# A transformer block whose instruction order and PSUM banks come from a stored table

## The chip, the cores and the metric

The kernel runs on one core of a Trainium2 chip. The metric is the device time of one execution in microseconds, as the median of several runs. The engines are TensorE (PE), VectorE (DVE), ScalarE (ACT) and GpSimd (POOL); SyncE (SP) issues the DMA transfers. PSUM, into which PE writes, has eight banks here called 0 to 7.

## The reference

One pre-layer-norm transformer block: attention with a sliding window, then a gated feed-forward network (FFN). Everything is float32; S = 2048 tokens, D = 448, 16 heads of 28, window W = 256, FFN width 1792.

```python
def _A_ref(x, wqkv, wo):                 # x: (1, 2048, 448)
    qkv = (x @ wqkv).reshape(B, S, 3, H, Dh).transpose(2, 0, 3, 1, 4)
    q, k, v = qkv[0], qkv[1], qkv[2]
    scores = einsum("bhqd,bhkd->bhqk", q, k) * Dh ** -0.5
    mask = (i - j >= 0) & (i - j < W)
    p = softmax(where(mask, scores, -1e9))
    o = einsum("bhqk,bhkd->bhqd", p, v)
    return o.transpose(0, 2, 1, 3).reshape(B, S, D) @ wo

def _B_ref(x, w_gate, w_up, w_down):
    return (gelu(x @ w_gate) * (x @ w_up)) @ w_down

h  = x + _A_ref(layernorm(x), A_wqkv, A_wo)
h2 = h + _B_ref(layernorm(h), B_w_gate, B_w_up, B_w_down)
```

## The kernel before

**How the program is made.** The kernel isn't written in the order in which it runs. Python functions record 6,036 operations in a list `L` (class `Lists`): each has an engine (`pe`, `dve`, `act`, `pool`, `sp`, or `py` for steps that only mark a point), an assumed cost and latency, a key, the data that it reads and writes, and the PSUM banks that it uses, at first as abstract `Bank` objects of a kind. By engine they are 3,324 for PE, 998 for DVE, 890 for ACT, 400 for POOL and 419 for SP. One operation may emit several instructions: an `attend` emits all its small matmuls.

**What sets the order.** `Lists.run` (L141) is a list scheduler: it keeps a clock for each engine, takes at each step the operation that can start earliest (by the key where several can), and gives an abstract bank a real one when its first operation starts, from those that `allowed` (L1534) names for its kind. Emission in this order fixes the order on each engine, since an engine's queue is in order, and it fixes the banks. `Lists.refine` (L338) runs this 110 times with changed keys and keeps the best by the model's time, `Lists.replay` (L253) adding random delays; `Lists.latest` (L291) computes late start times for new keys. All this happens while the kernel is built. Where the model shows a gap of more than 0.1 us on PE, `idle` (L1562) puts filler into it: transposes of the identity into a free bank (line L1573), allowed in the first 26 us of the model's time and from 235 to 330 us.

**The work.** Two passes p = 0, 1 over head groups, in each four chunks c of 512 tokens:
- `layer_norms` and `normalise`: statistics on DVE, scaling, PE transposes (L554), a split into a high and a low part. Matrix products use such high and low parts, so a product takes several matmuls; most are issued by the helper `mul` at line L496, and the splits stand at L499 (ACT) and L502 (DVE or POOL).
- `values` (matmuls of 224 columns) and `project_tile` (512 columns) make v, q and k; q and k go to DRAM and come back in another layout through `loads`, into the tile `ring`.
- `scores` (matmuls of 84 rows, read by DVE at L925 for row maxima), `maxima` (L952), `probs` (matmuls of 104 rows, read by ACT as exponentials at L997), `select` (POOL masks, L1008), `attend` (second products, L1027, banks 4 and 5), `drain`, and `output` (448 columns).
- the FFN: the first eight steps by `conv` and `down`, then `unit` and `down`. `unit` makes a two-by-two block of products from seven block products, with sums of token and weight blocks made by `combine` (DVE) and `record` (POOL, DVE). `down` accumulates groups on banks 4 to 7, read by DVE residual adds at L1297; `unit` uses banks 0 to 3.

In `allowed`, scores use banks 0 and 1 and probabilities banks 2 and 3 (bank 7 as well once the projections are through); the other products of attention use 6 and 7, and any that aren't in use yet or any more.

Of the kernel before, what the change touches and what calls it, by code (L numbers as in the profile page):

```python
# [62 lines left out]
SLOW = 9.0  # L63
WARM = 26.0
THIN = (235, 330)
# [3 lines left out]
WAKE = {"py": 0.0, "pe": 0.25, "dve": 0.025, "act": 0.025, "pool": 0.1, "sp": 0.02}  # L69
EASE = {"py": 0.0, "pe": 0.05, "dve": 0.04, "act": 0.04, "pool": 0.05, "sp": 0.02}  # L70


def mm(n):
    return max(n / 2400 + 0.004, 0.112)


ROUNDS = 110
SEED = 3
HEAT = 0.3
MIX = 0.8  # L80
COOL = 800
WIDE = 0.04
LATE = 0.015


class Op:
    __slots__ = ("eng", "cost", "lat", "key", "fn", "deps", "users", "left", "banks", "port", "ready", "start", "fin",
                 "size", "tag", "then", "took", "done", "rank")


class Bank:


    def __init__(self, kind):
        self.kind, self.k, self.left = kind, None, 0


class Lists:
# [3 lines left out]
    def __init__(self):  # L102
        self.ops, self.seen, self.open, self.all = [], {}, {}, {}

    def op(self, eng, cost, lat, key, fn, r=(), w=(), bank=None, port=False, size=0, tag=None, after=()):
        o = Op()
        o.eng, o.cost, o.lat, o.key, o.fn, o.port, o.size, o.tag = eng, cost, lat, key, fn, port, size, tag
        o.deps, o.users, o.ready, o.start = set(after), [], 0.0, None
        o.banks = () if bank is None else tuple(bank) if type(bank) is list else (bank,)
        for b in o.banks:  # L110
            b.left += 1
# [18 lines left out]
        for d in o.deps:  # L130
            d.users.append(o)
        self.ops.append(o)
        if tag is not None:
            self.open[tag] = self.open.get(tag, 0) + 1
            self.all.setdefault(tag, []).append(o)
        return o

    def fresh(self, tag):
        return self.open[tag] == len(self.all[tag])

    def run(self, allowed, idle, emit=False):  # L141

        E = ("py", "pe", "dve", "act", "pool", "sp")
        free = dict.fromkeys(E, START)
        free["py"] = 0.0
        lock = {"dve": 0.0, "pool": 0.0}
        bank_free = dict.fromkeys(range(8), 0.0)
        bus, dmas = 0.0, []
        cand = {e: [] for e in E}
        self.order = []  # L150
        self.open = {tag: len(l) for tag, l in self.all.items()}
        for i, o in enumerate(self.ops):
            o.left, o.ready, o.start, o.rank = len(o.deps), 0.0, None, (o.key, i)
            for b in o.banks:
                b.k, b.left = None, 0
            if not o.left:
                insort(cand[o.eng], (o.rank, o))
        for o in self.ops:
            for b in o.banks:
                b.left += 1  # L160
        n = len(self.ops)

        def start_of(e, o):
            t = max(free[e], o.ready)
            if o.port:
                t = max(t, lock["pool" if e == "dve" else "dve"] - 0.03)
            if e == "sp" and len(dmas) >= 8:
                t = max(t, dmas[-8])
            got = []
            for b in o.banks:  # L170
                if b.k is None:
                    ks = [k for k in allowed(b.kind) if bank_free[k] is not None]
                    if not ks:
                        return None, None
                    k = min(ks, key=lambda k: max(t, bank_free[k] + WAKE[e]))
                    t = max(t, bank_free[k] + WAKE[e])
                    got.append((b, k))
            return t, got

        def choice(e):  # L180
            found, now, most = [], free[e], None
            for _, o in cand[e]:
                if most is not None and o.ready > most:
                    continue
                t, got = start_of(e, o)
                if t is not None:
                    found.append((t, o, got))
                    if most is None or t + EASE[e] < most:
                        most = t + EASE[e]
                    if t <= now:  # L190
                        break
            return next((f for f in found if f[0] <= most), None)

        picks, stale = {}, set(E)
        while n:
            best = None
            for e in E:
                if e in stale:
                    picks[e] = choice(e)
                c = picks[e]  # L200
                if c is not None and (best is None or c[0] < best[0]):
                    best = c
            stale = set()
            if best is None:
                return None
            t, o, got = best
            e = o.eng
            if e == "pe" and t > free["pe"] + 0.1:
                until = idle(free["pe"], t, bank_free, emit)
                if until:  # L210
                    free["pe"] = until
                    stale = set(E)
                    continue
            del cand[e][bisect_left(cand[e], (o.rank,))]
            stale.add(e)
            if o.banks or o.tag is not None:
                stale |= {"pe", "dve"}
            if o.port:
                stale |= {"dve", "pool"}
            for b, k in got:  # L220
                b.k = k
                bank_free[k] = None
            o.start = t
            cost, lat = o.cost, o.lat
            if e == "sp":
                bus = max(bus, t + 1.2) + o.size * 0.0034 + (1.25 if len(dmas) == 2 else 0)
                lat = bus + 0.7 - t
                dmas.append(t + lat)
            if e == "pe" and t < SLOW:
                cost, lat = 2 * cost, lat + cost  # L230
            free[e] = t + cost
            o.fin = t + lat + (MARGIN if e == "sp" and t > 15 else 0)
            if o.port:
                lock[e] = t + cost
            self.order.append(o)
            if emit:
                o.fn()
            if o.tag is not None:
                self.open[o.tag] -= 1
            n -= 1  # L240
            for b in o.banks:
                b.left -= 1
                if not b.left:
                    bank_free[b.k] = max(o.fin, t + cost)
            for u in o.users:
                u.left -= 1
                u.ready = max(u.ready, o.start + cost if e == u.eng == "pe" else o.fin + WAKE[u.eng])
                if not u.left:
                    insort(cand[u.eng], (u.rank, u))
                    stale.add(u.eng)  # L250
        return max(o.fin for o in self.ops)

    def replay(self, rnd):  # L253

        E = ("py", "pe", "dve", "act", "pool", "sp")
        free, lock = dict.fromkeys(E, START), {"dve": 0.0, "pool": 0.0}
        bus, dmas, gone = 0.0, [], {}
        for o in self.order:
# [119 lines left out]
def block_kernel(ctx: ExitStack, tc, x, wqk_in, wv_in, wo_in, ffn_in, halves_in, out):  # L378
# [1155 lines left out]
    def allowed(kind):  # L1534
# [23 lines left out]
        if what == "att":  # L1558
            return [4 + i]
# [76 lines left out]
```

## Time and profile before

| | |
|---|---|
| median of 3 runs | 686.2 us (685.5 to 686.44) |
| span of the profiled execution, first to last instruction | 684.9 us |
| instructions | 12,356 |
| DMA | 89.67 MB, mean 131 GB/s |
| chain that ended last | PE 87%, DVE 6%, ACT 3%, DMA 2%, issue 1% |

The profiled execution's span lies 1.3 us under the median of the runs; the profile records no other time for it. "Busy" is the union of an engine's instruction intervals. PEld are weight loads, which run beside matmuls. A row of a group gives the line, engine, operation, names and shapes, then count, busy time, mean ns of one instruction, and idle time before them with what ended it. All names of matmul operands are those of tiles (`ring`, `proj`, `xT`, `wos`), whatever they hold at the time.

### The profile page before, as it was taken

How to read it: one execution, taken by the hardware profiler on the slowest of the kernel's cores; microseconds unless marked ns; L12 is line 12 of the kernel's file. 1: busy time of each engine (PE TensorE's matmuls, PEld its weight loads, DVE VectorE, ACT ScalarE, POOL GpSimd, SP SyncE). 2: the span in 40 equal slices, each digit the busy share in tenths (PEclk: the TensorE clock that was granted, in tenths of full speed). 3: DMA queues.
4: the chain of work that ended last, by engine and by line, in shares of the span. 5: the costliest groups of instructions: out<-in, count | busy, mean ns of one | idle time of the engine just before them, and what ended most of it. 6: DMA issues, size and time to landing. Idle time of an engine off the chain costs nothing.

```text
span 684.9 us, 12356 instructions
## 1 busy us (share of the span) xinstructions
PE 675.0 (99%) x4128; PEld 596.7 (87%) x4128; DVE 503.1 (73%) x1274; ACT 418.5 (61%) x908; POOL 295.9 (43%) x462
## 2 busy tenths in 40 slices
PE   8999999999999999999999999999999999999997
PEld 7898888888888888778998899899999999999997
DVE  7968979866587867884899998877667745645544
ACT  7758777776767788796555665644554543533331
POOL 5702544343445667645524465254654631501100
PEclk9999999999999999999999999999999999999999
DMA  8798655566547597633533432212112210111102
GB/s 289 230 304 265 224 190 177 164 186 199 178 143 226 162 248 202 170 75 84 152 87 103 117 108 75 85 53 78 65 53 91 66 53 15 38 53 68 54 1 107
DMA packets 92951, 89.67 MB, mean 131 GB/s; under 512 B 35224, under 2 KB 82008, under 8 KB 92888
## 3 DMA queue, kind: packets, MB, share of 16 engines
q1 hardware_dynamic: 92888, 88.89, 42.4%
q8 instruction: 32, 0.52, 0.3%
q14 instruction: 31, 0.25, 0.1%
HBM read 59.51 MB, written 29.36 MB: 130 GB/s over the span
## 4 chain that ended last, share of the span: by engine, by line
PE 87%; DVE 6%; ACT 3%; DMA 2%; issue 1%; POOL 0%; SPq 0%; DVEq 0%; ACTq 0%
PE bank L496 80%; PE bank L1027 6%; PE bank L554 1%; DVE X L502 1%; ACT ring L499 1%; DVE v L694 1%; DMA v<-xn 1%; DVE proj L502 1%; DMA q<-proj 1%; ACT xT L499 1%; DVE xT L502 1%; ACT proj L499 0%; ACT pp L997 0%; DVE mt L1342 0%; DVE bnst L531 0%
## 5 line engine op out<-in xcount | busy, mean ns | idle before, releaser
L496 PE MATMUL bank<-xT,proj 128*128 128x512 f32 x620 | 177.5, 384 | 0.0
L496 PE MATMUL bank<-ring 84*128 84x384 f32 (+5 forms) x618 | 155.1, 314 | 1.3 <-ACT pp L997 0.7
L925 DVE CUSTOM_DVE_ANT_0 mt<-bank,mt 128x384 bf16<-128x384 f32 (+2 forms) x256 | 129.0, 526 | 35.4 <-PE bank L496 30.3
L997 ACT ACTIVATE pp<-bank 128x384 f32<-128x384 f32 (+2 forms) x352 | 123.5, 389 | 44.6 <-PE bank L496 41.2
L496 PE MATMUL bank<-xT,ring 128*128 128x512 f32 x536 | 134.9, 380 | 0.2 <-ACT bank L1248 0.2
L496 PEld LDWEIGHTS bank<-ring 104*128 104x128 f32 (+2 forms) x618 | 109.6, 190 | 22.4 <-issue 5.8
L496 PE MATMUL bank<-ring,proj 128*128 128x448 f32 x628 | 127.5, 353 | 1.4 <-DVE hres L1297 1.4
L1008 POOL TENSOR_SCALAR_AFFINE_SELECT pp<-pp 128x512 f32<-128x512 f32 x120 | 74.6, 635 | 116.1 <-ACT pp L997 104.4
L496 PEld LDWEIGHTS bank<-xT,proj 128*128 128x128 f32 x620 | 113.7, 190 | 10.5 <-issue 0.4
L496 PEld LDWEIGHTS bank<-ring,proj 128*128 128x128 f32 x628 | 118.6, 189 | 4.5 <-ACT xT L499 1.8
L496 PEld LDWEIGHTS bank<-xT,ring 128*128 128x128 f32 x536 | 101.0, 189 | 13.7 <-ACT bank L1248 0.6
L1297 DVE TENSOR_TENSOR hres<-bank,hres 128x448 f32<-128x448 f32 x72 | 41.3, 622 | 26.8 <-PE bank L496 26.7
L496 PE MATMUL bank<-proj,xT 128*128 128x224 f32 x352 | 60.2, 276 | 0.3 <-DVE xT L502 0.2
L1259 ACT ACTIVATE v<-v 128x512 f32<-128x512 f32 x24 | 15.1, 630 | 69.9 <-DVE v L1241 69.9
L502 POOL TENSOR_TENSOR ring<-raw,ring 128x256 fp32r<-128x256 f32 (+2 forms) x42 | 38.4, 920 | 44.3 <-ACT ring L499 36.1
L496 PEld LDWEIGHTS bank<-proj,xT 128*128 128x128 f32 x352 | 53.3, 191 | 1.8 <-ACT proj L499 0.4
L1165 POOL TENSOR_TENSOR v<-raw 128x256 f32<-128x256 f32 x18 | 15.3, 851 | 87.0 <-DMA raw<-in_halves_dram 39.7
L502 DVE TENSOR_TENSOR proj<-v,proj 128x512 fp32r<-128x512 f32 (+1 forms) x56 | 44.0, 792 | 8.9 <-ACT proj L499 7.6
L496 PE MATMUL bank<-wos,ohl 128*128 128x448 f32 x192 | 50.2, 363 | 0.0
L499 ACT ACTIVATE proj<-v 128x512 fp32r<-128x512 f32 (+1 forms) x56 | 33.5, 601 | 24.3 <-DVE v L1267 13.5
L496 PE MATMUL bank<-X,ring 128*128 128x512 f32 x146 | 48.2, 379 | 0.0
L1165 POOL TENSOR_TENSOR raw<-raw 64x128 f32<-64x128 f32 (+1 forms) x90 | 46.3, 527 | 2.2
(116 smaller groups left out, 999.4 us busy)
## 6 DMA issues: line engine op xcount, KB each, us to landing
ring<-k SPq DMA_DIRECT2D x44, 336.0 KB
raw<-in_halves_dram SPq DMA_DIRECT2D x18, 640.0 KB
ring<-q SPq DMA_DIRECT2D x32, 336.0 KB
q<-proj SPq DMA_DIRECT2D x15, 448.0 KB
k<-proj SPq DMA_DIRECT2D x11, 448.0 KB
hres<-in_x_dram SPq DMA_DIRECT2D x16, 224.0 KB
xn<-xn SPq DMA_DIRECT2D x64, 56.0 KB
mt<-in_halves_dram SPq DMA_DIRECT2D x16, 224.0 KB
```

Of the source, the lines that this page charges most:

```text
L496: nc.tensor.matmul(o.rearrange("p (t h) -> p t h", h=2), w, mixed(m), **how)
L499: nc.scalar.activation(dst, src, AF.Copy)
L502: (eng or nc.vector).tensor_sub(dst, src, f(hi))
L554: nc.tensor.transpose(bank[b.k][:, n * 128:(n + 1) * 128], xn[i2][:, o:o + 128], ident)
L694: op("dve", 0.07 + n * 0.00104, 0.17 + n * 0.00104, key, lambda: nc.vector.tensor_tensor(out, a, b, op=op_), [*ar, *br, "mtfree"], w, port ...
L925: nc.vector.tensor_tensor_reduce(plain(junk[s % 2][:, o:384]), unmixed(bank[b.k][:, o:384]), plain(mask[:, o:384]), 1.0, -BIG, OP.add, OP. ...
L997: nc.scalar.activation(plain(pp[:, j, o * 128:o * 128 + n]), unmixed(bank[b.k][:, 0:n]), AF.Exp, scale=SCALE)
L1008: nc.gpsimd.affine_select(a, a, pattern=[[0, 4], [-cm, 128]], compare_op=op_, fill=0.0, base=0, channel_multiplier=cm)
L1027: nc.tensor.matmul(bank[b.k][32 * j:32 * j + DH + 1, lo * 128:(hi + 1) * 128], v[:, 4 * c - 2 + m, g % 2, j, :], pp[:, j, at[m] * 128:(at[ ...
L1165: op("pool", 0.14 + n * 0.00215, 0.18 + n * 0.00215, key, lambda: nc.gpsimd.tensor_tensor(out, a, b, op=OP.subtract), [*ar, *br], w, port= ...
L1259: op("act", 0.485, 0.608, key + 11, lambda: nc.scalar.activation(A, A, AF.Gelu_apprx_tanh), ta, ta)
L1297: op("dve", 0.533, 0.626, key + 3 * q + 3, lambda t=t, b=banks[q]: nc.vector.tensor_tensor(plain(hres[:, t, :]), unmixed(bank[b.k][:, 0:D] ...
```

## The change

`run`, `replay`, `latest`, `refine`, `allowed` and `idle` go, with their constants and the clocks of class `Op`. The functions that record the operations stay. A new method `play` reads a stored table, `PLAN`: 16-bit words, first one bank for each of the 926 bank groups in the order of recording, then the order. A word below 6,036 is the number of an operation, which is emitted; one above is a filler transpose into that bank.

```diff
+    def play(self, plan, warm):
+
         n = len(self.ops)
...
+        words = memoryview(zlib.decompress(base64.b85decode(plan))).cast("H")
+        banks = list(dict.fromkeys(b for o in self.ops for b in o.banks))
+        for b, k in zip(banks, words):
+            b.k = k
+        done = set()
+        for w in words[len(banks):]:
+            if w >= n:
+                warm(w - n)
+                continue
+            o = self.ops[w]
+            assert o.deps <= done
+            o.fn()
+            done.add(o)
+        assert len(done) == n
...
-    L.refine(allowed, idle)
-    L.run(allowed, idle, True)
+    def warm(k):
+        nc.tensor.transpose(bank[k][:, 0:128], ident, ident)
+
+    L.play(PLAN, warm)
```

The recorded costs change in two places (`mm(n)` loses its floor of 0.112 us, and `project_tile` its added 0.002 us), but nothing reads costs any more.

What the table holds, read off by decoding its words against the recorded list, beside the order and banks of before:

| | before | table |
|---|---|---|
| filler transposes | 84 | 32 |
| of these behind the 119th PE operation or filler | 49 | 0 |
| PE order from the first `unit` product on (1,524 operations) | | the same, place by place |
| neighbours kept in the order: PE, DVE, ACT, POOL, SP | | 2,001 of 3,323; 173 of 997; 149 of 889; 140 of 399; 70 of 418 |
| median and largest move in the order: DVE, ACT, POOL, SP | | 2 and 37; 2 and 53; 1 and 17; 2 and 30 |
| banks of the 256 scores | 0 and 1 in 250, 7 in 6 | 0 to 3, 6 and 7 in 31 to 52 each |
| banks of the 352 probability products | 2 and 3 in 329, 7 in 23 | 0 to 3, 6 and 7 in 39 to 69 each |
| a score's bank used last by a probability product, or the reverse | 7 | 245 |
| five or fewer PE instructions (operations and fillers) between a bank's last writer and the next group in it: scores | 24 | 51 |
| the same: probability products | 131 | 62 |
| banks of `attend`, `down` and `unit` | | the same |

In the table's order, residual adds of `down` in the later FFN stand in DVE's queue behind up to 3.7 us (by the recorded costs) of other DVE work that comes after their last matmul; in the order of before there is none for most of them.

434 lines of the change are left out of this document (142 added, 292 removed).

## The prediction

> **What bounds the kernel now.** I read the page's first lines, then stretches of the span, then the instructions of single stretches by their shape.
>
> ```profile
> span 684.9 us, 12356 instructions
> PE 675.0 (99%) x4128; PEld 596.7 (87%) x4128; DVE 503.1 (73%) x1274; ACT 418.5 (61%) x908; POOL 295.9 (43%) x462
> ```
>
> PE looks busy for 99% of the span, which would leave 9.9 us to any reordering. That reading is wrong here: a matmul counts as busy until its modelled end, and two that overlap hide the wait between their starts. So I ask how much time the matmuls of a stretch need when they follow each other closely, and compare that with the stretch. The next fence has four stretches, with busy time and counts of each engine, then the granted clock.
>
> ```profile
> 80.00:140.00 60.00, 60.00 (x465) 51.31 (x464) 51.73 (x169) 44.80 (x115) 26.06 (x36) 1.00 0.59 192
> 235.00:330.00 95.00, 93.70 (x695) 76.40 (x694) 69.66 (x208) 77.82 (x198) 59.33 (x84) 1.00 0.59 156
> 330.00:380.00 50.00, 48.50 (x238) 44.11 (x236) 45.72 (x113) 27.27 (x50) 18.96 (x31) 1.00 0.42 116
> 380.00:680.00 300.00, 299.88 (x1459) 275.41 (x1460) 200.95 (x343) 142.80 (x257) 113.31 (x176) 1.00 0.20 62
> ```
>
> From 380 us PE has 0.12 us of idle time in 300 us, and DVE, the next engine, is 67% busy. A closely packed piece of it, by the timeline (start, length, instructions), and one group of the attention's second products from the chain of waits:
>
> ```profile
> 406.44 2.43 PE L496 MATMUL bank<-ring,proj 128*128 128x448 f32 x12
> 408.71 1.03 PE L496 MATMUL bank<-xT,proj 128*128 128x512 f32 x4
> 409.57 0.38 PE L496 MATMUL bank<-X,proj 128*128 128x512 f32 x1
> 248.77 1.43 PE bank L1027 x24
> ```
>
> Twelve matmuls of 448 columns start in 408.71 - 406.44 = 2.27 us, 0.189 us each; four of 512 in 0.86 us, 0.215 each. Both are 0.422 ns a column. A second product costs 1.43 / 24 = 0.060 us. With these two prices, the end of attention, where output products and the first FFN products run beside it:
>
> ```profile
> L496 PE MATMUL bank<-xT,proj 128*128 128x512 f32 x114 | 32.3, 385 | 0.0
> L496 PE MATMUL bank<-ring 84*128 84x384 f32 x59 | 19.6, 355 | 0.2
> L496 PE MATMUL bank<-wos,ohl 128*128 128x448 f32 x72 | 17.7, 363 | 0.0
> L496 PE MATMUL bank<-ring 104*128 104x384 f32 x39 | 13.4, 361 | 0.8 <-ACT pp L997 0.7
> L496 PE MATMUL bank<-ring 104*128 104x256 f32 x36 | 10.2, 301 | 0.2
> L1573 PE MATMUL bank<-ident 128*128 128x128 f32 x46 | 8.9, 275 | 0.0
> L1027 PE MATMUL bank<-pp,v 128*29 128x384 f32 x80 | 8.4, 491 | 0.0
> L496 PE MATMUL bank<-ring 104*128 104x128 f32 x36 | 8.3, 253 | 0.1
> L496 PE MATMUL bank<-proj,xT 128*128 128x224 f32 x44 | 7.8, 277 | 0.0
> L1027 PE MATMUL bank<-pp,v 128*29 128x256 f32 x80 | 6.1, 379 | 0.0
> L1027 PE MATMUL bank<-pp,v 128*29 128x128 f32 x80 | 4.1, 278 | 0.0
> L952 PE MATMUL bank<-one,mhl 128*72 128x128 f32 x8 | 1.9, 239 | 0.0
> L496 PE MATMUL bank<-proj 128*128 128x448 f32 x1 | 0.4, 352 | 0.0
> ```
>
> Columns without L1573 and L1027: 114 x 512 + 98 x 384 + 73 x 448 + 44 x 224 + 36 x 256 + 44 x 128 = 153,408, or 64.8 us. The 240 second products add 14.3 us. PE needs 79.1 of these 95 us and **loses 15.9 us, 17%**. Line L1573, 46 transposes of the identity, is filler in that lost time, not work. The same count in the middle of attention:
>
> ```profile
> L496 PE MATMUL bank<-xT,proj 128*128 128x512 f32 x62 | 20.1, 385 | 0.0
> L496 PE MATMUL bank<-ring 84*128 84x384 f32 x61 | 19.9, 339 | 0.0
> L496 PE MATMUL bank<-wos,ohl 128*128 128x448 f32 x48 | 13.2, 363 | 0.0
> L496 PE MATMUL bank<-ring 104*128 104x384 f32 x32 | 10.2, 334 | 0.0
> L496 PE MATMUL bank<-proj,xT 128*128 128x224 f32 x44 | 7.8, 273 | 0.0
> L496 PE MATMUL bank<-ring 104*128 104x256 f32 x27 | 7.7, 290 | 0.0
> L1027 PE MATMUL bank<-pp,v 128*29 128x384 f32 x48 | 5.0, 491 | 0.0
> L496 PE MATMUL bank<-ring 104*128 104x128 f32 x24 | 4.8, 234 | 0.0
> L1027 PE MATMUL bank<-pp,v 128*29 128x256 f32 x56 | 4.3, 381 | 0.0
> L1027 PE MATMUL bank<-pp,v 128*29 128x128 f32 x56 | 2.9, 277 | 0.0
> L952 PE MATMUL bank<-one,mhl 128*72 128x128 f32 x7 | 1.6, 228 | 0.0
> ```
>
> 62 x 512 + 93 x 384 + 48 x 448 + 44 x 224 + 27 x 256 + 31 x 128 = 109,696 columns are 46.3 us, the 160 second products 9.5. PE needs 55.8 of 60 us and **loses 4.2 us, 7%**, though no row shows idle time. For all of 60 to 235 us I scale that by 175 / 60: 12 us, an estimate. A part of it is no wait at all, but changes of shape that cost more than their columns.
>
> **The change, part by part.** It moves the whole program's order, so I cost it by stretch.
>
> The tail, from the first FFN `unit`: the table's PE order is that of before, place by place, for all 1,524 operations, and the banks of `down` and `unit` are the same. PE is back to back there. Gain 0. What is reordered is DVE, ACT, POOL and SP around it. Their cover is DVE's 99 us of idle time in 300; in the table several residual adds of `down` stand behind more DVE work than before, so if the cover fails they hold up the next group's banks. Bound: 0 to 3 us lost; I take 0, which is nearest to the 0.12 us of before.
>
> 235 to 330 us: the 46 fillers here and the few after them go (84 become 32, and those 32 stand in the first part of the program). Taken out alone they gain nothing, since they fill a wait; their cover is the wait. The gain must come from new banks and order. The lower bound of this stretch is 79.1 us by PE, and 77.8 us by ACT, nearly the same, so PE can't be packed here as in the tail. If the stretch lost only the 7% of mid-attention it would take 79.1 / 0.93 = 85 us, a gain of 10. ACT would then be 77.8 / 85 = 92% busy, against 75% in mid-attention, so all of that is too much; I take 7. Ends: 0 (every wait stays, without its filler) and 12 (ACT 94% busy).
>
> 60 to 235 us: here score and probability products go from two banks each, plus bank 7 late, to a common pool of six. Counting in the two orders the PE instructions that stand between a bank's last writer and its next user: five or fewer for 131 of the probability products before, for 62 after; for the score products 24 before and 51 after. Together 155 become 113, 27% fewer close reuses. If the 12 us lost are such waits, 27% is 3.2 us. I take 3. Ends: 6 (the probability products set the pace, and halve) and -3 (the score products set it, since DVE is the busier engine, 86% against ACT's 75%).
>
> 330 to 380 us: PE stands once, for the residual adds that free a `down` bank:
>
> ```profile
> 364.37 1.94 PE L496 MATMUL bank<-ring,proj 128*128 128x448 f32 x9 [1.45 <-DVE hres L1297]
> ```
>
> DVE is 91% busy in this stretch, PE's work between the two `down` groups is unchanged, and the table puts three of the four adds nearer their matmuls in DVE's queue and one farther. Of 1.45 us I take 0.5; ends 0 and 1.5.
>
> Before 60 us: the first 22 fillers, the transposes and the first value products come as before, with three fillers fewer. Gain 0, ends -1 and 2; it hangs on input DMAs that the table can move by little. On SP's queue, whose 419 transfers move by a median of 2 places and at most 30, a transfer of projected rows is on the chain once, 3.86 us:
>
> ```profile
> 238.30 3.86 DMA q<-proj
> ```
>
> That path gets neither longer nor shorter by any count I can make; it lies within the ends of its stretch.
>
> Sum: 0 + 7 + 3 + 0.5 + 0 = 10.5 us, span 684.9 - 10.5 = 674.4. The median of the three runs is 686.2, 1.3 above the profiled span; with the same 1.3 **I predict 675.7 us**.
>
> **A rule that speaks against it.** The fillers were in the code to keep TensorE awake. Their first run and a late one:
>
> ```profile
> 1.45 4.36 PE L1573 MATMUL bank<-ident 128*128 128x128 f32 x22 [1.45 <-POOL ident L757]
> 328.26 2.24 PE L1573 MATMUL bank<-ident 128*128 128x128 f32 x19
> ```
>
> The first takes 0.198 us for each, the late one 0.118. So PE starts slow; one slow spell of this kind costs 22 x 0.08 = 1.8 us. The Trainium skill, "TensorE: Matmul & The Clock Gate", section "Part 1: The HAM clock gate", says that the array runs at half clock until it has been busy for a window of about 3.4 us, and falls back after an idle window of that length. The trace agrees on the slow start; the granted clock is 1.00 in all four stretches, so no run here shows the fall. By the rule alone a wait would have to grow past 3.4 us to matter, and the sum would then be 1.8 us worse for each.
>
> **The rivals.**
> 1. *Little of the lost time was banks.* If the waits around 235 to 330 us are chains through DMA and ACT (the 3.86 us above), the new order gains what the fillers' stretch gives with one such transfer better hidden, 3.9 us: 682. For it: ACT's 77.8 us leave little. Against: the waits lie scattered, 46 fillers in many places.
> 2. *No change.* The lost time is switching cost of shapes, which any order pays: 686. Against: 17% lost in one stretch and 7% in another with the same shapes.
> 3. *Slower: banks now tie ACT and DVE together.* Before, a score or probability product followed one of the other kind in its bank 7 times; after, 245 times. Then a late ACT, which frees probability banks, also holds up score products, and DVE behind them. PE's price of such a wait is in this row (total, times, longest):
>
> ```profile
> PE bank L496 <- ACT pp L997: 0.7, 2, 0.5
> ```
>
> 0.35 us each. From 10.5 / 0.35 = 30 of the 238 further mixed reuses the gain is gone; at 50 the time is 675.7 + 17.5 = 693. Against: close reuses fall.
> 4. *A cold clock.* With the fillers gone, PE stands long enough in several places that the slow spell returns. It needs six spells, 6 x 1.8 us, to undo the gain; at eight the time is 690. Against: the longest PE wait of before, outside the start, is 1.45 us.
> 5. *The lost time mostly goes.* All upper ends, 12 + 6 + 1.5 + 2 = 21.5: 665.
>
> **How the numbers follow.** Forecast (gain 6 to 16, 670 to 680): 0.58. Rival 1: 0.17. No change, within 0.2% (1.4 us, about what a measurement of this kernel can tell from none): 0.06. Rival 3: 0.09. Rival 4: 0.02. Rival 5: 0.08. Faster is 0.58 + 0.17 + 0.08 = 0.83; same 0.06; slower 0.11. The range goes from rival 5's 665 to 685.5, past rival 1; it leaves out the slower cases, most of no change, and what lies below 665, about 0.2.
>
> **What the changed profile would show.** L1573 with 32 instructions, the last before 60 us. The step at 235 to 330 us is right if the same shapes there (the stretch from the start of the p = 1 tail to the last output product) take 85 to 90 us with ACT near 90% busy; wrong if waits `PE <- ACT pp` add up to several us, or ACT's share stays at 82%. The step on banks is right if mid-attention loses nearer 5% than 7%. The tail is right if the stretch from the first `unit` product on keeps its length to within 1 us; if `PE <- DVE hres` shows there, the deferred adds are the cause. A granted clock under 1.00 would show rival 4. The whole is wrong if PE's order was limited by ACT's and DVE's own in-order queues, so that fewer close bank reuses move no start.

## The result, and the profile after

The changed kernel takes **682.2 us** (median; 681.85 to 683.07) against 686.2 for the kernel before: a ratio of 0.9942, with a 95% interval from 0.9928 to 0.9956. It is faster by 4.0 us, where 10.5 were forecast. The profiled execution has a span of 681.0 us, 3.9 less than before; this execution itself took 683.07 us.

The first lines of the page of the changed kernel:

```profile
span 681.0 us, 12237 instructions
PE 669.8 (98%) x4076; PEld 591.2 (87%) x4076; DVE 491.9 (72%) x1274; ACT 413.2 (61%) x908; POOL 296.5 (44%) x462
```

The 52 fewer matmuls are the fillers. PE's busy share falls by a point while the kernel gets faster, so it says as little as it did before. The same four stretches as in the prediction (bounds and length; then busy time and count for PE, PEld, DVE, ACT and POOL; granted clock, DMA share, GB/s), for the changed kernel:

```profile
80.00:140.00 60.00, 60.00 (x465) 51.06 (x464) 49.68 (x167) 45.55 (x116) 26.37 (x36) 1.00 0.65 192
235.00:330.00 95.00, 94.39 (x686) 77.47 (x685) 75.21 (x225) 80.07 (x203) 65.61 (x94) 1.00 0.62 163
330.00:380.00 50.00, 47.56 (x226) 41.72 (x225) 44.81 (x110) 27.63 (x52) 18.34 (x29) 1.00 0.43 115
380.00:680.00 300.00, 296.33 (x1440) 271.79 (x1440) 188.10 (x339) 134.83 (x251) 110.84 (x173) 1.00 0.20 64
```

The fourth row's 3.7 us without PE are mostly the kernel's end, which now falls into it: after the last matmul, at 677 us, only adds and output transfers are left. Only the second row has visibly more in it: DVE 75.2 us against 69.7 in the same 95 us, POOL 65.6 against 59.3, ACT 80.1 against 77.8. PE's own share there has to be counted by shape, as in the prediction. The groups of matmuls from 235 to 330 us in the changed kernel (count, then busy time and mean ns of one, then idle time before them):

```profile
L253 PE MATMUL bank<-xT,proj 128*128 128x512 f32 x110 | 31.3, 387 | 0.1
L253 PE MATMUL bank<-ring 84*128 84x384 f32 x60 | 19.5, 354 | 0.1
L253 PE MATMUL bank<-wos,ohl 128*128 128x448 f32 x72 | 17.4, 360 | 0.0
L253 PE MATMUL bank<-ring 104*128 104x384 f32 x40 | 11.8, 344 | 0.0
L253 PE MATMUL bank<-ring 104*128 104x256 f32 x36 | 9.9, 299 | 0.0
L253 PE MATMUL bank<-proj,xT 128*128 128x224 f32 x51 | 8.5, 271 | 0.0
L784 PE MATMUL bank<-pp,v 128*29 128x384 f32 x80 | 8.4, 491 | 0.0
L253 PE MATMUL bank<-ring 104*128 104x128 f32 x36 | 7.9, 238 | 0.0
L784 PE MATMUL bank<-pp,v 128*29 128x256 f32 x80 | 6.1, 379 | 0.0
L253 PE MATMUL bank<-proj 128*128 128x448 f32 x24 | 5.0, 357 | 0.2 <-DVE proj L259 0.2
L784 PE MATMUL bank<-pp,v 128*29 128x128 f32 x80 | 4.1, 278 | 0.0
L253 PE MATMUL bank<-xT,ring 128*128 128x512 f32 x9 | 2.1, 379 | 0.0
L709 PE MATMUL bank<-one,mhl 128*72 128x128 f32 x8 | 1.9, 235 | 0.1
```

Without the second products (L784) these are 119 x 512 + 100 x 384 + 96 x 448 + 51 x 224 + 36 x 256 + 44 x 128 = 168,608 columns, 71.2 us by the prediction's 0.422 ns; with 240 second products, 14.3 us, the work is 85.5 of 95 us. Before it was 79.1. PE now loses 9.5 us in this stretch instead of 15.9: **6.4 us came from here**.

That is more than the whole gain, so something was given back. To find it I paired each PE operation with itself in the other trace, by its operands and its number in order, and took the difference of the starts. The last matmuls of attention and its output products start 5 us earlier than before, those at 335 to 360 us 6.5 us earlier, the first `unit` product 5.3 us earlier, and everything from 455 us on 3.9 us earlier. So 1.2 us are lost between 355 and 367 us, and 1.4 in the FFN's tail. The timeline of the changed kernel shows the two kinds of place (start, length, instructions; in brackets the idle time before and what ended it):

```profile
357.74 1.14 DVE L1054 TENSOR_TENSOR hres<-bank,hres 128x448 f32<-128x448 f32 x2
358.49 3.12 PE L253 MATMUL bank<-ring,proj 128*128 128x448 f32 x12 [1.90 <-ACT xT L256]
...
379.88 1.13 PE L253 MATMUL bank<-xT,ring 128*128 128x512 f32 x4 [0.47 <-DVE v L998]
430.11 1.13 PE L253 MATMUL bank<-xT,ring 128*128 128x512 f32 x4 [0.50 <-ACT v L1002]
```

In the second row PE stands 1.90 us before a `down` group. The profile names an ACT split, `xT`; but by the order and the banks it is the first of the two residual adds (L1054) in the row above, the pair running from 357.74 to 358.88 us, that frees the bank of the group's first product. The other two rows are places in the tail that had no wait before: a `unit` product waits for its bank, once for a DVE add and once for an ACT copy.

By the prediction's own prices of a column and a second product, counted between the same operations in both traces, PE's lost time is:

| stretch | before | after | gain | forecast |
|---|---|---|---|---|
| start | | | 0.3 | 0 |
| 60 to 235 us | 17.1 | 17.1 | 0.0 | 3 |
| 235 to 330 us | 16.3 | 9.7 | 6.6 | 7 |
| 330 to 380 us | 2.2 | 3.6 | -1.4 | 0.5 |
| from 380 us | | | -1.4 | 0 |

The gains add to 4.1 us, beside 3.9 in the span. Two questions follow. Why did 27% fewer close reuses of banks gain nothing from 60 to 235 us? And is what was lost from 330 us on due to the table's order of DVE work?

### The profile page after: what moved, and what is told of

Read it like the earlier page. It is cut to its first block, busy times and chain, and to the rows that moved or that the text cites. A ratio compares the mean times of both kernels' runs of the same rounds, so it can differ in the third digit from the quotient of the medians.

```text
span 681.0 us, 12237 instructions
## 1 busy us (share of the span) xinstructions
PE 669.8 (98%) x4076; PEld 591.2 (87%) x4076; DVE 491.9 (72%) x1274; ACT 413.2 (61%) x908; POOL 296.5 (44%) x462
## 4 chain that ended last, share of the span: by engine, by line
PE 85%; DVE 8%; DMA 3%; ACT 2%; issue 1%; SPq 0%; POOL 0%; DVEq 0%; ACTq 0%; POOLq 0%
PE bank L253 78%; PE bank L784 6%; DVE X L259 1%; DVE v L451 1%; DVE proj L259 1%; DMA raw<-in_halves_dram 1%; DMA hres<-in_x_dram 1%; DMA v<-xn 1%; PE bank L311 1%; DVE mt L682 1%; PE bank L709 0%; DVE hres L1054 0%; DVE xT L259 0%; ACT xT L256 0%; DVE ring L259 0%
## 5 line engine op out<-in xcount | busy, mean ns | idle before, releaser
L253 PE MATMUL bank<-xT,proj 128*128 128x512 f32 x620 | 180.4, 386 | 0.1
L682 DVE CUSTOM_DVE_ANT_0 mt<-bank,mt 128x384 bf16<-128x384 f32 (+2 forms) x256 | 129.9, 527 | 39.7 <-PE bank L253 32.8
L253 PE MATMUL bank<-ring 84*128 84x384 f32 (+5 forms) x618 | 148.1, 310 | 0.5 <-DVE mx L682 0.3
L754 ACT ACTIVATE pp<-bank 128x384 f32<-128x384 f32 (+2 forms) x352 | 121.2, 388 | 39.1 <-PE bank L253 31.3
L259 POOL TENSOR_TENSOR ring<-raw,ring 128x256 fp32r<-128x256 f32 (+2 forms) x42 | 38.8, 932 | 69.3 <-ACT ring L256 64.5
L253 PE MATMUL bank<-proj,xT 128*128 128x224 f32 x352 | 67.5, 271 | 0.0
L1054 DVE TENSOR_TENSOR hres<-bank,hres 128x448 f32<-128x448 f32 x72 | 42.6, 617 | 25.4 <-PE bank L253 25.3
L253 PEld LDWEIGHTS bank<-proj,xT 128*128 128x128 f32 x352 | 57.4, 191 | 2.3 <-DVE mx L682 0.6
L259 DVE TENSOR_TENSOR proj<-v,proj 128x512 fp32r<-128x512 f32 (+1 forms) x56 | 39.7, 717 | 26.2 <-ACT proj L256 26.1
L998 DVE TENSOR_TENSOR v<-v,bank 128x512 f32<-128x512 f32 x48 | 32.8, 684 | 34.8 <-PE bank L253 31.6
```

The source lines that it names most:

```text
L253: nc.tensor.matmul(o.rearrange("p (t h) -> p t h", h=2), w, mixed(m), **how)
L259: (eng or nc.vector).tensor_sub(dst, src, f(hi))
L682: nc.vector.tensor_tensor_reduce(plain(junk[s % 2][:, o:384]), unmixed(bank[b.k][:, o:384]), plain(mask[:, o:384]), 1.0, -BIG, OP.add, OP. ...
L754: nc.scalar.activation(plain(pp[:, j, o * 128:o * 128 + n]), unmixed(bank[b.k][:, 0:n]), AF.Exp, scale=SCALE)
L998: op("dve", 0.605, 0.702, key, lambda: nc.vector.tensor_tensor(plain(out), plain(a), unmixed(bank[bs[i].k]), op=OP.add), ar, w, bs[i])
L1054: op("dve", 0.533, 0.626, key + 3 * q + 3, lambda t=t, b=banks[q]: nc.vector.tensor_tensor(plain(hres[:, t, :]), unmixed(bank[b.k][:, 0:D] ...
```

## The experiments

All kernels below but one are the changed kernel with another `PLAN`; the diffs show decoded words. "The table" is the changed kernel's plan; "before's order" is the order and the banks of the kernel before, written as such a plan. Ratios are against the kernel before, timed beside it on the same chip, with its median at 686.1 to 686.5 us; so a few tenths of a us between two sections mean nothing.

### The fillers alone

```diff
 before's order, 84 filler words
-the 49 filler words behind the 119th PE word
 all other words as they are
```

> The kernel before with the 49 filler transposes of its middle part left out, nothing else changed (order and banks of all operations as before). Theory A (fillers stand in waits of PE that are there anyway): within 0.7 us of 686.2, granted clock 1.00. Theory B (the fillers keep the clock up): the granted clock falls under 1.00 somewhere between 250 and 330 us and the time rises by 1.8 us for each slow spell, so 688 or more. Theory C (the fillers themselves cost PE time): 2 us or more faster, and then this alone would be half of the table's gain.

Measured: 687.76 us (686.42 to 688.86), ratio 1.0022 [1.0014, 1.0031]. The windows of its trace around the place where the granted clock (third column from the end) falls:

```profile
274.60:278.00 3.40, 2.70 (x19) 1.70 (x11) 3.40 (x12) 2.62 (x8) 3.32 (x5) 1.00 1.01 260
278.00:284.80 6.80, 6.67 (x21) 5.51 (x20) 3.42 (x15) 2.56 (x7) 3.02 (x7) 0.50 0.93 243
284.80:292.00 7.20, 7.20 (x57) 5.68 (x56) 6.18 (x21) 5.54 (x15) 2.27 (x3) 1.00 0.24 45
```

For 6.8 us the clock is granted at half speed. What went before it is not a long wait: in the 3.4 us from 274.6 on the longest wait of PE is 0.7 us, PE counts as busy for 2.7 of them, and by column prices it streams for about 40%. DVE, POOL and DMA are full there, and PE works in short pieces beside them. So in the old order the fillers had a use, and the theory of the clock holds, though its 688 us was just missed. By the pairing PE falls 2.2 us behind the kernel before between 250 and 300 us, of the 3.4 us that half speed for 6.8 us could cost; by the medians the loss is 1.6 us. The runs scatter with the clock: the only one with a mean granted clock of 1.000 took 686.45 us, the five at 0.997 or 0.998 took 686.4 to 687.9, the five at 0.994 or 0.995 took 686.6 to 688.9.

The changes of the clock in this trace, at 4.93, 278.00 and 284.83 us, lie on a grid of 3.413 us (80 steps, then 2), and the stretch from 274.6 us on is one step of it. Another step of the same trace left the clock at full, though PE counts as busy for less of it and stands 1.66 us in one piece:

```profile
329.20:332.61 3.41, 1.75 (x10) 1.40 (x9) 3.41 (x9) 1.72 (x4) 3.13 (x3) 1.00 0.51 144
```

By the columns of the matmuls that start in it, PE streams for 44% of this step. In the next section's kernel a step at 41% (282.5 to 285.9 us) was followed by half speed, and in the one after it a step at 44% (277.5 to 280.9 us, in attention, fillers counted) was not. From these few steps I estimate that the line lies between 41 and 44% of streaming; busy time doesn't tell.

The Trainium skill, "TensorE: Matmul & The Clock Gate", section "Part 1: The HAM clock gate", gives a window of about 3.4 us and half clock after an idle one. The 6.8 us agree with two such windows; its table of states speaks of idle windows alone, while here PE was at work in the window that was followed by half clock.

Without the fillers the profile also names what their longest run in the kernel before, 19 of them from 328.26 us on, stood in: a wait for a DVE split (L259) ahead of the first FFN products of 448 columns. That wait in this kernel, then in the changed one:

```profile
PE bank L253 <- DVE proj L259: 1.7, 1, 1.7
PE bank L253 <- DVE proj L259: 0.2, 1, 0.2
```

So about 1.5 of the 6.6 us gained from 235 to 330 us come from a DVE operation that the table puts earlier, and not from a bank.

The table runs at full clock with no filler there. Against the old order without fillers its gain is 5.5 us (687.8 to 682.2); leaving out the fillers gains nothing by itself.

### Banks of the table's kind in the old order

The prediction's count says that a common pool of six banks leaves fewer close reuses. Here only the banks of scores, probabilities and row maxima change, by the rule "the bank that has been free longest".

```diff
 before's order without the 49 fillers; 486 of 926 bank words, the first four:
-bank[16..19] = 0 1 0 1
+bank[16..19] = 3 0 1 2
```

> Order of before, without the 49 fillers; only the banks of score, probability and row-maximum products change: instead of two each (and bank 7 late) each takes the one of banks 0, 1, 2, 3, 6 and 7 that has been free longest. Close reuses (five or fewer PE instructions between) fall from 34 to 21 for scores and from 146 to 44 for probabilities. Matching starts and ends in the two traces operation by operation, waits of PE on a bank came to 7.2 us between 235 and 330 us before, but to only 2.6 us between 60 and 235 us. Theory A (banks held PE up in the late stretch): 3 to 6 us faster than the kernel without fillers, 680 to 683, nearly all of it after 235 us. Theory B (the order was the table's merit, and a PE that gets a bank sooner only waits for ACT or DVE elsewhere): under 1 us.

Measured: 694.94 us (691.45 to 695.49), ratio 1.0118 [1.0099, 1.0137], outside both theories: 7.2 us slower than the same order with the old banks, although close reuses fell from 34 to 21 for scores and from 146 to 44 for probabilities (without fillers to count between them, the old banks' 24 and 131 are 34 and 146). The chain of waits for this kernel (engine and line, what it waited for: us in total, times, longest):

```profile
PE bank L253 <- DVE mx L682: 3.2, 8, 0.6
PE bank L253 <- ACT pp L754: 1.0, 4, 0.4
```

PE now waits for DVE's row maxima (L682) in eight places. Pairing the operations shows who waits: value products about 2.3 us, projections 2.0, outputs 1.5, all for banks 6 and 7, which scores and probabilities now hold. My count looked only at scores and probabilities, and took no notice of the products that lost their own two banks. The theory behind the count falls here. The clock is a part of the 7.2 us: the two runs with a granted clock of 0.999 or more took 691.5 and 692.3 us, against 686.45 for the old banks at 1.000, so 5 to 6 us are left to the banks.

### Sharing four banks in the old order

To take that out, scores and probabilities here share only their own four banks.

```diff
 before's order with all fillers; 447 of 926 bank words, the first four:
-bank[16..19] = 0 1 0 1
+bank[16..19] = 3 0 1 2      (rotation over 0, 1, 2, 3)
```

> Order of before with all its 84 fillers; only those score, probability and row-maximum products that had banks 0 to 3 now share these four, each taking the one that was given back first; banks 6 and 7 stay with the projections, values and outputs. In the pool of six, which was 7 us slower than the same order without it, the trace showed waits of value, projection and output products for banks that scores and probabilities held. Theory A (it was that loss of their own banks): no such waits, and probabilities gain from close reuses that fall: 683 to 686. Theory B (sharing a bank between products that DVE frees and products that ACT frees costs by itself): 688 or slower, with waits of probabilities on DVE.

Measured: 687.66 us (686.98 to 688.38), ratio 1.0020 [1.0011, 1.0028], between the two theories. The waits of PE from 235 to 330 us:

```profile
PE bank L253 <- ACT pp L754: 1.4, 3, 0.8
PE bank L253 <- DVE mx L682: 0.5, 2, 0.3
```

By pairs of last reader and next user of each bank, a probability product waits 2.5 us for ACT instead of 4.6, and a score product 0.8 for DVE instead of 1.8: the sharing does relieve both. But probability products now wait 2.6 us for DVE instead of 0.1, and `conv` products 1.4 for ACT instead of 0.05. What sharing relieves, the ties between ACT and DVE take back.

### The old separation in the table's order

The reverse: the table's order, with scores kept to banks of their own wherever one is free at that place in the order.

```diff
 the table's order; 523 of 926 bank words, the first three:
-bank[17..19] = 2 0 2
+bank[17..19] = 1 3 7
 scores from 0, 1, 7; probabilities and row maxima from 2, 3, 6; 40 of 640 fall back to any free bank
```

> The table's order; only the banks of score, probability and row-maximum products change: scores take from 0, 1 and 7, the others from 2, 3 and 6, the one given back first, and any free bank where the order leaves none (40 of 640). Theory A (order and banks of the table were found together and each is worth little without the other): 3 us or more slower than the table's 682.2. Theory B (the order carries the gain): 681.5 to 683.5.

Measured: 714.94 us (713.7 to 715.79), ratio 1.0416 [1.0400, 1.0432]: 33 us slower than the table. From 60 to 235 us PE loses 32.6 us by the pairing, and 20.2 from 235 to 330, where the table lost 17.1 and 9.7. The chain of waits of this kernel:

```profile
PE bank L253 <- DVE mx L682: 5.2, 14, 0.6
PE bank L253 <- ACT pp L754: 3.5, 15, 0.4
```

Both kinds of product now wait, in 14 and 15 places. A bank assignment isn't good or bad by itself: a separation of the old kind costs 33 us in the new order, and a pool of the new kind 7 us in the old order. Each of these assignments follows one simple rule; whether one that was made for its order would do better, no run shows.

### What a short matmul costs

The other part of the question: how much of the lost time is waiting at all? This kernel has only streams of matmuls of one or two shapes, with four weights and four banks in rotation and nothing to wait for.

```diff
-(the whole block)
+    def mul(n, rows):
+        i = k[0] % 4
+        k[0] += 1
+        nc.tensor.matmul(bank[i][:, 0:n]..., w[i][0:rows], m[0:rows, 0:n]..., start=True, stop=True)
+    stream((512,), 60); stream((128,), 60); stream((224,), 60); stream((256,), 60)
+    stream((384,), 60); stream((128, 448), 40); ...
```

> Leaves the whole block out: streams of matmuls alone, float32 round mode with new weights for each, no reader and so no wait: 60 each of 512, 128, 224, 256 and 384 columns, then pairs of 128 with 448, 512 and 384, then mixed rows as in attention, 512-column streams between them. It prices the shapes that the prediction priced at 0.422 ns a column. Theory A (short matmuls are held by their weight loads): 128 columns take about 0.11 us instead of 0.054, 224 about 0.11 instead of 0.095, and a pair of 128 with 448 some 0.05 us more than its 0.243; mid-attention's 31 matmuls of 128 and 44 of 224 columns then explain 2 to 3 of its 4.2 us lost in 60. Theory B (columns alone count): 0.054, 0.095 and 0.243, and the lost time is waits for other engines.

Its span is 175.2 us. The windows of its trace, with 5 us each of 128, 224, 256 and 384 columns, and 10 us of 128 and 448 in turn (the first count is that of the matmuls; it takes in one or two that overlap the edges):

```profile
22.00:27.00 5.00, 5.00 (x47) 5.00 (x47) 0.00 (x0) 0.00 (x0) 0.00 (x0) 1.00 0.01 3
33.00:38.00 5.00, 5.00 (x48) 5.00 (x46) 0.00 (x0) 0.00 (x0) 0.00 (x0) 1.00 0.00 0
44.00:49.00 5.00, 5.00 (x47) 5.00 (x46) 0.00 (x0) 0.00 (x0) 0.00 (x0) 1.00 0.00 0
55.00:60.00 5.00, 5.00 (x33) 5.00 (x32) 0.00 (x0) 0.00 (x0) 0.00 (x0) 1.00 0.01 3
69.00:79.00 10.00, 10.00 (x68) 10.00 (x68) 0.00 (x0) 0.00 (x0) 0.00 (x0) 1.00 0.00 0
```

128, 224 and 256 columns all come at the same rate, though one has twice the columns of another. From start to start it is 0.111 to 0.112 us for these three, 0.1625 for 384 and 0.216 for 512. (PEld counts as busy throughout at 384 columns too, so its share alone doesn't tell.) A pair of 128 and 448 takes 0.301 us, 0.058 more than the 0.243 of its columns, so a long neighbour hides none of what the short one costs. In it the long matmul starts 0.056 us behind the short one, and the next short one 0.245 us later; so 0.11 us isn't a floor for every start. Weight loads of 128, 72 and 29 columns last 189, 143 and 107 ns in the trace of before, so a load grows with its columns. The theory of the weight load fits all of this, and the theory of columns alone is out.

The mixed rows cost little: in the stream, matmuls of 384, 384 and 512 columns with 84, 104 and 128 rows take 0.551 us together, where their prices add to 0.540. In the kernel before, a 128-column matmul of probabilities between longer ones costs the same 0.06 us over its columns as in the stream.

With the price of a weight load the prediction's count can be mended. In mid-attention it had 31 matmuls of 128 columns, 44 of 224 and 27 of 256; they cost 0.058, 0.0175 and 0.004 us more than by columns, 1.8 + 0.8 + 0.1 = 2.7 of the 4.2 us "lost". From 60 to 235 us the lost time becomes 7.6 us before and 7.7 after; from 235 to 330 us 12.9 and 6.2, so the gain there is untouched. By these prices, and leaving out what stands behind second products, PE before has one gap over 0.2 us from 60 to 235 us, and 95 gaps of 0.05 to 0.2 us that add to 7.2 us; with the table these are 2, and 107 that add to 7.4 us. What makes the small ones stays open in part. From 235 us to the split at 330 us the gaps over 0.2 us go from 14 to 4, and from 6.9 us to 1.1.

The Trainium skill, "TensorE: Matmul & The Clock Gate", section "Back-to-back issue gap", gives 2.4 columns a ns and 2.5 ns more for a single matmul, and for sustained streams about 81 ns at 128 columns and 131 ns at 512. The first fits the streams here at 512 (0.216 us); the sustained figures don't fit these float32 streams, which take 112 and 216 ns. Its section "LDWEIGHTS (loading the stationary operand)" gives 107 ns by its formula for a load of 128 columns of weights, which is near the 111 to 112 measured from start to start.

### The table's first part undone

```diff
-the table's words
+before's order up to the operation that starts at 226.07 us (no fillers behind the first 35), then the rest in the table's order
 bank words of each part from the plan that gives its order
```

> Order and banks of before (without mid fillers) up to the operation that started at 226 us, then the table's order and banks for all that is left. In the two traces the attention products up to there start 0 to 2 us later with the table, and all of its gain comes after. Theory A (the table's first part is worth nothing by itself): 680 to 682.5, as fast as the whole table or up to 2 us faster. Theory B (its first part prepares the second, by doing ACT and POOL work early): 684 or slower.

Measured: 681.32 us (680.69 to 682.44), ratio 0.9934 [0.9922, 0.9945]. The table's first 226 us bring nothing: with the old order there the kernel is, if anything, 0.9 us faster, and the ratios' intervals overlap. Theory A is right.

### The table's last part undone

```diff
 the table's words up to the first unit product
-the rest in the table's order
+the rest in before's order
```

> The table's order up to the first unit product (361 us), then the order of before for all that is left; PE's order in the tail is the same in both, so only DVE, ACT, POOL and SP change places. In the trace of the table PE waits in the tail four times where before waited once or less: 0.6 us at 380 us, 0.7 at 430, 0.3 at 439, each for DVE or ACT. Theory A (the table's order of DVE and ACT in the tail gives back 1.2 to 1.7 us): 680.5 to 681 against the table's 682.2. Theory B (the tail's waits come from state that the earlier part leaves behind, as transfers or splits that are late): 682 or more.

Measured: 681.32 us (680.70 to 682.64), ratio 0.9934 [0.9922, 0.9946]. That lies between the theories, nearer to A. By the pairing PE's waits in the tail fall by about 1 us. PE's order is the same in both, so what is gained is due to the order of DVE, ACT, POOL and SP there; the ratios' intervals overlap, so the 0.9 us aren't certain by themselves.

### Only the middle

```diff
-the table's words
+before's order to 226 us, the table's order to the first unit product, before's order from there
```

> Order of before up to 226 us, the table's up to the first unit product, the order of before for the tail: the two halves that each gained 0.9 us on the table alone. If they add, 680.4 (682.2 - 0.9 - 0.9); if the two gains were one and the same, or chance, 681.3 or more.

Measured: **680.74 us** (680.34 to 681.56), ratio 0.9912 [0.9898, 0.9926], the fastest of all and clear of the table's interval: near the 680.4 of two corrections that add. The windows of this kernel:

```profile
235.00:330.00 95.00, 94.27 (x682) 77.14 (x681) 75.20 (x224) 80.18 (x202) 65.62 (x94) 1.00 0.64 164
355.50:358.90 3.40, 1.99 (x10) 1.32 (x9) 3.34 (x8) 1.94 (x4) 0.00 (x0) 1.00 0.74 231
```

The first row is that of the table to within 0.4 us on every engine. So **the whole gain lies between 226 and 367 us**; outside it the table costs about 1.5 us. The second row is the stop ahead of the `down` group, with DVE busy for 3.34 of 3.40 us and PE streaming about 44% by prices. The clock did not fall behind it.

### The stop at 358 us: adds first

DVE is full there, and some combine steps for later `unit` products stand ahead of the adds.

```diff
 DVE's queue ahead of the wait at 358 us (table)
+add q0, split for conv, add q1, add q2, add q3
 eight combine and record steps
-add q0, split for conv, add q1, add q2, add q3      (interleaved with them)
```

> The table's kernel with one change in DVE's queue: the four residual adds that free the banks of the third-last down group before the unit stage (and one split that the group needs) go ahead of eight combine and record operations. PE waited 2.1 us there at 358 us, with DVE busy without a gap from 340 to 362 us. Theory A (DVE's backlog is the limit; the first unit products need what was put back): the wait moves on to the unit products, within 0.7 us of the table's 682.2. Theory B (only the order of the adds is the fault): 680 to 680.7.

Measured: 683.04 us (682.91 to 683.65), ratio 0.9947 [0.9934, 0.9961], 0.8 us more than the changed kernel (theory A allowed 0.7), with the ratios' intervals overlapping. The chain of waits of this kernel:

```profile
PE bank L253 <- DVE xT L259: 0.8, 1, 0.8
PE bank L253 <- DVE X L259: 0.4, 1, 0.4
PE bank L253 <- ACT bank L1005: 0.4, 1, 0.4
```

The 1.90 us wait of the `down` group is gone, and the first `unit` products wait instead, at 359.4, 362.0 and 362.9 us: the sums that they need (L259) are the ones pushed back. By the pairing PE is 2.9 us ahead of the changed kernel near 358 us and has lost all of it by 370 us. The wait moved, as theory A had it.

### The stop at 358 us: adds first, layer norm of two tiles later

```diff
 as above, and
-8 DVE steps of two late token tiles, with their POOL, ACT and SP followers, between 320 and 356 us
+the same behind 361 us
```

> The same adds put forward, and eight DVE operations (3.4 us by their recorded costs: statistics and transposes of two late token tiles, which PE first needs near 436 us) with what follows them on ACT, POOL and SP put behind the combine operations, from 326 to 353 us to after 361 us. Theory A (DVE's load before the first unit product is the limit): the wait at 358 us goes and does not come back at the unit products, 680 to 681. Theory B (the wait isn't DVE's load, or the late tiles then come too late and PE waits near 430 us): 682 or more.

Measured: 692.92 us (692.38 to 693.94), ratio 1.0090 [1.0077, 1.0103]. The edit failed for a reason of its own, which the timeline of ACT shows:

```profile
364.80 0.76 ACT L306 ACTIVATE xn<-hres,bnve 128x448 f32<-128x448 f32 x1 [2.28 <-POOL bnve L285]
366.28 0.76 ACT L306 ACTIVATE xn<-hres,bnve 128x448 f32<-128x448 f32 x1 [0.71 <-DVE xn L345]
366.94 0.58 ACT L1005 ACTIVATE bank<-bank 128x512 f32<-128x512 f32 x1
```

The two normalising steps (L306) moved with their tiles and now stand in ACT's queue, where they wait for POOL and DVE; behind them waits the copy between banks (L1005) on which the `unit` products hang. PE stood 4.9 and 3.7 us, and the clock went to half for 10.2 us. It says nothing on whether DVE's load sets the stop.

### The stop at 358 us: only the statistics later

```diff
 the only-the-middle kernel, with adds first, and
-the DVE statistics of two late token tiles ahead of the adds
+the same at about 363 us (the steps that follow from them stay behind)
```

> The kernel of three parts (680.7), with the four adds forward as before and only the statistics of two late token tiles (1.5 us of DVE by recorded costs) put back from 328 to 339 us to about 363 us, their POOL step to about 365 us; the ACT step that needs it stays at 369 us, so that nothing stands in front of the gelu in ACT's queue as it did in the version that took 692.9 us. Theory A (DVE's load before the first unit product is the limit): 679 to 680. Theory B (it isn't, or freed DVE time is lost again): 680.5 or more.

Measured: 683.29 us (682.88 to 683.69), ratio 0.9956 [0.9944, 0.9968], 2.5 us slower than the kernel that it was made from. PE in the timeline:

```profile
359.15 0.92 PE L253 MATMUL bank<-xT,proj 128*128 128x512 f32 x3 [0.84 <-DVE xT L259]
362.00 0.48 PE L253 MATMUL bank<-X,proj 128*128 128x512 f32 x1 [0.64 <-DVE X L259]
363.73 1.13 PE L253 MATMUL bank<-xT,proj 128*128 128x512 f32 x4 [1.24 <-ACT bank L1005]
```

Again the first `unit` products wait, here for DVE's sums and for ACT, which itself had waited for DVE. Taking load off DVE ahead of the stop didn't free it, as theory B had it. The rows fit a chain of combine steps from DVE through ACT and back to DVE that sets the start of the `unit` products, but no run isolates that chain; and the adds and the statistics were moved together, so what each cost isn't shown. What would remove the wait stays open.

## Why the prediction was right and wrong

**235 to 330 us (forecast 7, measured 6.6): right.** The count by shape found the stretch, its bound and the size. PE did 85.5 us of work in 95; the 79.1 us of before would take 88 at that rate, within the 85 to 90 named. ACT went to 84% busy, short of 90%, and the waits of probability products for ACT fell from 4.6 us to 0.7; about 1.5 us more is the DVE split at 330 us. That the fillers alone are worth nothing held too, to within 1.6 us on the wrong side. What the prediction didn't see is that new banks alone don't bring it: three kernels with only the banks changed, in either order, were slower.

**60 to 235 us (forecast 3, measured 0): wrong, and the step that failed.** It said "if the 12 us lost are such waits, 27% is 3.2 us". They weren't. 9.5 of the 17.1 us that the count gives for the whole stretch are weight loads of matmuls of up to 256 columns, which the table has as well, and bank waits of before come to 2.6 us by the pairing, with the table to about as much. The test that the prediction named went against it too: from 80 to 140 us the table loses 4.5 of 60 us by the same count, 7.6%, and not nearer 5%. The warning stood in the text (changes of shape that cost more than their columns) and wasn't used in the sum. The count of close reuses failed as a measure too: it fell by two thirds in the pooled kernel, which was 7.2 us slower. Of the 6.4 us by which the terms were too good, 3 are this step, 1.9 the stretch to 380 us and 1.4 the tail.

**The tail (forecast 0, bound 0 to 3, measured -1.4): the bound held, the value was too good.** Same PE order and same banks didn't mean the same time: the two largest waits are for `unit` banks, freed by DVE and ACT late. The prediction named the residual adds of `down` as the cause; they were not.

**330 to 380 us (forecast 0.5, ends 0 and 1.5, measured -1.4): wrong sign.** The old wait for an add (1.45 us) was replaced by one of 1.90 with an add in front, and moving the adds ahead moved the wait on. The ends left out that PE's part of the stretch arrives 6.5 us earlier, while DVE's operations of 346 to 366 us come only 3.4 to 5.0 us earlier by the pairing (medians).

**Before 60 us (forecast 0, measured 0.3)** held: the trace of the kernel with the tail undone, which has the table's order there, is 0.4 us ahead of the table's from 12 us on, so the 0.3 us say nothing.

**The rivals.** The time of rival 1 came out, 682, but not its reason: bank waits were lost time from 235 to 330 us, and were gained, and the 4.0 us are a gain of 6.6 less what was given back. Around its transfer, from 238 to 244 us, PE's gaps over 0.2 us before add to 0.7 us, not 3.9. The fillers weren't as scattered as the prediction said against it: 19 of the 46 stood in the one wait for the split. Rival 2, switching cost, is true in the form of weight loads of most of mid-attention and not of the later stretch. Rival 3, that shared banks tie ACT and DVE, is true of the banks alone, at 1.4 us for four shared banks and 7.2 for six; in the table order and banks go together. Rival 4, the cold clock, is true of the old order without fillers, with one spell that costs about the 1.8 us named (1.6 by the medians, 2.2 by the pairing), and not of the table, whose granted clock is 1.00 throughout. What spoke against it, that the longest wait of before is 1.45 us, left out the waits that fillers cover, up to 2.0 us.

## What to carry to other kernels

Price each matmul by the larger of its columns and its weight load before calling time lost, and pair operations across two traces instead of comparing windows: only then do a gain in one stretch and its return in the next separate. Banks and order are one choice; a count of bank reuses that left out who else needs the bank, and in which queue its reader stands, didn't predict the time here. Where a stored schedule is better in one stretch and worse in others, take the stretch: the middle alone gave 680.7 us, the whole table 682.2.

## What the hardware showed that I had not expected

Matmuls of 128, 224 and 256 columns with fresh weights all start 0.111 to 0.112 us apart, and a 448-column neighbour hides nothing of it. The granted clock went to half for 6.8 us after 3.4 us in which PE still streamed for 40% of the time with no wait over 0.7 us (and in another kernel at 41%), while steps of the same grid at 44% left it at full, one of them with PE standing 1.66 us in one piece.
